# Blockwise linear attention and a two-layer product on one core: two more block products in seven multiplications, copies into the second bank, and loads that cast

## The chip, the cores and the metric

The kernel runs on one core of a Trainium2 chip. The core has a matrix engine (TensorE, PE in the profile; its weight loads are listed as PEld), three engines for everything else (VectorE or DVE, ScalarE or ACT, GpSimd or POOL), a queue engine (SyncE or SP), and 16 DMA engines that move data between the chip's memory (HBM) and the on-chip memory (SBUF). Products are written to eight banks of a small accumulator memory (PSUM, 2 KB per partition and bank). The metric is the device time of one execution, in microseconds.

## The reference

Inputs are q, k, v of 4 batches, 8 heads, 768 positions and 64 features, a decay per head, and two weight matrices. Cut to what matters:

```python
for b in range(12):                       # blocks of 64 positions
    intra = (qb @ kb.T) * Dmask           # lam ** (i - j) for i >= j
    out_b = intra @ vb + (qb * lam_pow) @ kv_state
    kv_state = lam ** 64 * kv_state + (kb * rev_pow).T @ vb
x = out.transpose(0, 2, 1, 3).reshape(3072, 512)
h = x @ w_in                              # 512 x 2048
return (h * sigmoid(h)) @ w_out           # 2048 x 512
```

## The kernel before

A block of the kernel is 128 positions (two of the reference's), so there are 6 blocks times 4 batches, 24 units of 128 rows, numbered by rank: block n of batch b is 4n + b from block 2 on, and blocks 0 and 1 of a batch stand together as units 0 to 7. Attention works on sets of two units: sets 0 to 3 are the paired blocks 0 and 1 of one batch, sets 4 to 11 are blocks 2 to 5, two batches each.

Per set the kernel loads k, q and v as float32 (`load_set`, L338, on SP's queue, 512 KB each, pieces of 256 bytes from block 2 on), casts k and q to bfloat16 (`cast`, L587, four quarter casts of 128x512 per set on ACT or DVE, into a buffer `kq`), scales v (`scale_v`), and turns k and q to feature-major form `kqT`. Sets 0 to 3 are turned on PE by transposes against an identity (eight transposes into one bank, then two copies out of it). Sets with `si >= TURNED` (4) are turned by a DMA transpose on SP's queue (`dma_turn`, L621). Then a burst of small matmuls gives states and scores (`first_part`), DVE masks the scores and updates the running state, and a second burst (`second_part`) gives the attention output, which DVE scales into `xt`, the right-hand side of the first product. From set 6 on, the second part of one set and the first part of the next go in one burst, which needs six PSUM banks at once.

The first product (`product1`, L813) multiplies w_in with one block of the four batches: 16 column blocks, four matmuls of 512 columns each, and a silu on ACT into tiles `g`. The last block (5) has a form with fewer multiplications instead (`product1_spared`, L906): both operands are split 2x2, seven products of sums take the place of eight products (Strassen's scheme in Winograd's form). Sums of weight quarters (`sums_of_w_in`) and of xt (T1 to T4) are made on DVE. In each of four column groups the seven products go to two banks, P and R. Products that are needed twice are copied from P to SBUF (`keep`) and added later by DVE (`total_of`).

The second product has a plain form, one unit at a time (`product2_plain`, L849, four pieces of four matmuls of 512 columns), for the first PLAIN units, and the seven-product form (`product2` and `products_of`, from L1010) for four units at a time, in pieces of sixteen matmuls of 256 columns. Sums of the left operand are on DVE, the fourth on POOL (`BY_POOL`); sums of w_out quarters are made once, and one of them (T1) overwrites a quarter of w_out, so it comes after all plain products. The last four units are done in two halves.

The order on all engines is made ahead of time by `Planner.order`, which simulates the engines: each task has a key (what is due first), an assumed duration on each engine that may do it, and buffers out of pools of fixed size (`POOLS`). A ready task goes to an engine if no other engine would end it earlier by the simulated times. `L320` in the profile is the helper of all tensor_tensor operations, `L313`, `L315` and `L317` that of copies on ACT, DVE and POOL. Keys of attention are LEAD (6.5) ranks ahead of its unit's first product. POOL's DMA issues (the weight loads, which cast to bfloat16) are chained in a fixed order, each held back by a one-column "gate" copy that waits for a load on SP's queue. Pools that matter here: eight banks; six `att` tokens, which limit the banks that attention and the pairs P, R hold at a time (a pair takes two); six `rb` buffers of 4 KB per partition for raw loads; three `kq`.

Of the kernel before, what the change touches and what calls it, by code (L numbers as in the profile page):

```python
# [37 lines left out]
class Planner:  # L38

    LAT = {"PE": 0.23, "ACT": 0.06, "DVE": 0.06, "POOL": 0.08, "SP": 0.0}  # L40
    BEGIN = {"PE": 0.8, "ACT": 8.3, "DVE": 4.5, "POOL": 4.7, "SP": 0.8}
    FIRST, LAST, AHEAD = {"SP": 1.9, "ACT": 1.15, "POOL": 2.5}, 1.0, 0.75
# [13 lines left out]
    def order(self):  # L56
# [63 lines left out]
        while len(out) < len(self.tasks):  # L120
# [9 lines left out]
            for e in free:  # L130
# [8 lines left out]
                while ready[e]:  # L139
# [12 lines left out]
                    mine = now + t.on[e]  # L152
                    if any(max(free[o], now) + d < mine - 1e-9 for o, d in t.on.items() if o != e):
                        kept.append((key, i, t))
                        continue
# [33 lines left out]
def kernel(  # L189
# [10 lines left out]
    nc = tc.nc  # L200
# [16 lines left out]
    FRESH, TURNED, ALONE, LEAD = 4, 4, 6, 6.5  # L217
    SEQUENCE = "s0 i0 s1 i1 i2 s2 i3 o0 s3 o1 o2 o3 s4"
    POOLS = dict(bank=8, ra=3, rb=6, kq=3, kqT=3, vd=3, st=3, xe=6, xf=3, y=2, yf=2,
                 xt2=2, xt4=2, g=18, s=12, m=3, osb=3, one=3, two=4, att=6)  # L220
    BY_POOL, IN_BY_POOL, PLAIN, SPARED = (4,), (), 8, 1
# [116 lines left out]
    def load_set(key, si):  # L338
        n, b = sets[si][0]
        nb = 2  # L340
        rs = [Buf("ra" if si in (0, 3) else "rb") for _ in range(3)]
# [11 lines left out]
        for i in range(3):  # L353
            ts.append([add((key, i), {"SP": 0.55}, lambda e, i=i: go(e, i), bufs=[rs[i]], nbytes=0.524,
                           kind=WIDE if n < PAIRED else SMALL, late=0.3 if si < FRESH else 3.0)])
# [54 lines left out]
    def key_of(si):  # L410
        u = rank[sets[si][0]]
        return u - 4.0 if sets[si][0][0] == 0 else u - LEAD
# [145 lines left out]
    def prepare(si):  # L558
# [7 lines left out]
        o.kq, o.kqT, o.vd, o.st = Buf("kq"), Buf("kqT"), Buf("vd"), Buf("st")  # L566
# [6 lines left out]
        def kq_of():  # L573
            return tile_of(o.kq, [128, nb, 2, NP, 2, 64], BF16, "kq")

        def kqT_of():
            return tile_of(o.kqT, [128, nb, 2, NP, U], BF16, "kqT")
# [9 lines left out]
        def cast(e, j, i):  # L587
            src = rs[i].tile[:, j * H:j * H + H, :].rearrange("p (m h) d -> p m h d", h=2)
            dst = kq_of()[:, j, i]
            copy(e, dst, src)  # L590

        ck = [[add((s - 1.0, i), {"DVE": 0.43, "ACT": 0.63}, lambda e, j=j, i=i: cast(e, j, i), deps=(lk, lq)[i],
                   bufs=[rs[i], o.kq]) for i in range(2)] for j in range(nb)]
        after("k", [t for ts in ck for t in ts])
# [10 lines left out]
        if si < TURNED:  # L605
            for j in range(nb):
                bank = Bank(fills=False)

                def turn(e, j=j, bank=bank):
                    t = tile_of(bank, [128, 2, NP, U], BF16, "tr")  # L610
                    for i in range(2):
                        for m in range(NP):
                            nc.tensor.transpose(t[:, i, m, :], kq_of()[:, j, i, m], ident)

                tr = add((s - 0.7, j), {"PE": 0.46}, turn, deps=ck[j], bufs=[bank, o.kq])
                for i in range(2):
                    o.turned.append(add((s - 1.0, 2), {"DVE": 0.43, "ACT": 0.6},
                                        lambda e, j=j, i=i, bank=bank: copy(e, kqT_of()[:, j, i], bank.tile[:, i]),
                                        deps=[tr], bufs=[bank, o.kqT]))
        else:  # L620
            def dma_turn(e):  # L621
                nc.sync.dma_start_transpose(kqT_of().rearrange("p b i m s -> p (b i m) s"),
# [550 lines left out]
```

## Time and profile before

| | |
|---|---|
| median of 3 runs | 208.62 us (208.38 to 209.31) |
| the profiled execution | 207.82 us, of which the profiled span is 206.1 us |
| TensorE busy | 187.0 us, 91% of the span |
| VectorE busy | 134.8 us, 65% |
| ScalarE busy | 107.4 us, 52% |
| GpSimd busy | 52.4 us, 25% |
| read from and written to HBM | 27.27 MB and 6.29 MB |

A page of the profile gives the busy time of each engine, the chain of work that ended last followed back from the end, the costliest groups of instructions by line and tile, and the DMA issues. "Idle before" a group is the time that its engine stood still ahead of it, with what ended that wait. Matmuls are pipelined and each record includes its way through the array, so the mean of a record (322 ns for a group) is longer than the step from one matmul to the next; steps are read from the chain, where sixteen matmuls of 256 columns take 1.75 us. The mean granted clock of TensorE is 0.989 of full speed.

### The profile page before, as it was taken

How to read it: one execution, taken by the hardware profiler on the slowest of the kernel's cores; microseconds unless marked ns; L12 is line 12 of the kernel's file. 1: busy time of each engine (PE TensorE's matmuls, PEld its weight loads, DVE VectorE, ACT ScalarE, POOL GpSimd, SP SyncE). 2: the span in 40 equal slices, each digit the busy share in tenths (PEclk: the TensorE clock that was granted, in tenths of full speed). 3: DMA queues.
4: the chain of work that ended last, by engine and by line, in shares of the span. 5: the costliest groups of instructions: out<-in, count | busy, mean ns of one | idle time of the engine just before them, and what ended most of it. 6: DMA issues, size and time to landing. Idle time of an engine off the chain costs nothing.

```text
span 206.1 us, 5719 instructions
## 1 busy us (share of the span) xinstructions
PE 187.0 (91%) x2445; PEld 132.9 (64%) x2464; DVE 134.8 (65%) x249; ACT 107.4 (52%) x195; POOL 52.4 (25%) x76
## 2 busy tenths in 40 slices
PE   0459399999999999999999999998999999999993
PEld 0347288786667565544578648474675778888882
DVE  6488632767950467716989953999758995665411
ACT  3637267874336453375734492745615453766420
POOL 7231400401130111222565013346003221222200
PEclk9999889999999999999999999999999999999999
DMA  3999999999999999999999999905101110102213
GB/s 99 292 253 260 228 222 265 235 199 214 228 238 249 156 216 231 238 219 195 263 213 234 203 213 240 244 7 117 39 3 54 51 54 0 54 0 102 88 52 118
DMA packets 88617, 33.92 MB, mean 165 GB/s; under 512 B 67088, under 2 KB 87568, under 8 KB 88592
## 3 DMA queue, kind: packets, MB, share of 16 engines
q1 hardware_dynamic: 79232, 23.60, 57.3%
q0 software_dynamic: 4224, 4.19, 12.2%
q10 hardware_dynamic: 5136, 5.77, 8.7%
q8 instruction: 19, 0.31, 0.7%
q14 instruction: 6, 0.05, 0.1%
HBM read 27.27 MB, written 6.29 MB: 163 GB/s over the span
## 4 chain that ended last, share of the span: by engine, by line
PE 82%; DMA 8%; DVE 7%; issue 1%; ACT 0%; POOL 0%; POOLq 0%; DVEq 0%
PE h_ps L830 31%; PE o_ps L1072 22%; PE o_ps L861 13%; PE h_ps L944 6%; DMA w_in_bf<-in_moe_w_in_dram 5%; DMA raw<-in_k_dram 3%; PE x_ps L687 2%; DVE s L320 2%; PE tr L442 2%; DVE g L320 1%; PE d_ps L647 1%; PE x_ps L679 1%; PE st_ps L657 1%; PE x_ps L538 1%; DVE kq L315 1%
## 5 line engine op out<-in xcount | busy, mean ns | idle before, releaser
L830 PE MATMUL h_ps<-xt,w_in_bf 128*128 128x256 bf16 (+1 forms) x439 | 75.7, 322 | 4.7 <-DMA w_in_bf<-in_moe_w_in_dram 3.3
L839 ACT ACTIVATE g<-h_ps 128x512 bf16<-128x512 f32 x80 | 47.1, 594 | 45.7 <-PE h_ps L830 45.0
L830 PEld LDWEIGHTS <-w_in_bf 128*128 128x128 bf16 x448 | 43.7, 99 | 30.1 <-DMA w_in_bf<-in_moe_w_in_dram 3.5
L861 PE MATMUL o_ps<-w_out_bf,g 128*128 128x512 bf16 x118 | 29.7, 379 | 0.6 <-issue 0.2
L320 POOL TENSOR_TENSOR s<-g,s 128x512 bf16<-128x512 bf16 x16 | 19.0, 1188 | 43.1 <-DVE s L320 26.8
L320 DVE TENSOR_TENSOR st<-st_ps,tri 128x512 bf16<-128x512 f32 x32 | 20.5, 681 | 11.2 <-PE st_ps L657 11.2
L1072 PEld LDWEIGHTS <-g 128*128 128x128 bf16 x256 | 24.9, 98 | 4.4 <-ACT g L839 0.3
L320 DVE TENSOR_TENSOR xt<-x_ps,lam_xe 128x512 bf16<-128x512 f32 x24 | 15.9, 699 | 15.2 <-PE x_ps L687 9.5
L1072 PEld LDWEIGHTS <-s 128*128 128x128 bf16 x192 | 18.7, 98 | 2.6
L861 PEld LDWEIGHTS <-g 128*128 128x128 bf16 x128 | 12.1, 98 | 12.0
L320 POOL TENSOR_TENSOR vd<-raw,lam_v 128x512 bf16<-128x512 f32 x10 | 13.3, 1334 | 25.1 <-DMA raw<-in_v_dram 19.7
L313 ACT ACTIVATE kq<-raw 128x512 bf16<-128x512 f32 x27 | 16.2, 621 | 2.1 <-DMA raw<-in_q_dram 1.6
L320 DVE TENSOR_TENSOR osb<-o_ps,m 128x512 f32<-128x512 f32 (+1 forms) x15 | 8.7, 583 | 10.9 <-ACT m L313 6.8
L1072 PE MATMUL o_ps<-wsum,g 128*128 128x256 bf16 x128 | 15.3, 272 | 0.0
L1072 PE MATMUL o_ps<-w_out_bf,s 128*128 128x256 bf16 x128 | 15.3, 273 | 0.0
L442 PE MATMUL tr<-ident,kq 128*128 128x128 bf16 x64 | 7.0, 260 | 8.8 <-POOL gate L331 6.9
L1072 PE MATMUL o_ps<-w_out_bf,g 128*128 128x256 bf16 x128 | 15.0, 273 | 0.0
L320 DVE TENSOR_TENSOR s<-g 128x512 bf16<-128x512 bf16 x16 | 8.2, 510 | 10.4 <-ACT g L839 6.6
L313 ACT ACTIVATE m<-o_ps 128x512 f32<-128x512 f32 (+1 forms) x14 | 7.0, 503 | 11.4 <-PE o_ps L1072 11.4
L320 DVE TENSOR_TENSOR vd<-raw,lam_v 128x512 bf16<-128x512 f32 x14 | 9.2, 681 | 5.0 <-DMA raw<-in_v_dram 5.0
L313 ACT ACTIVATE osb<-o_ps 128x512 f32<-128x512 f32 (+1 forms) x12 | 6.7, 562 | 10.4 <-PE o_ps L861 6.5
L315 DVE CAST kq<-raw 128x512 bf16<-128x512 f32 x21 | 9.1, 451 | 3.8 <-DMA raw<-in_k_dram 2.0
(88 smaller groups left out, 215.1 us busy)
## 6 DMA issues: line engine op xcount, KB each, us to landing
raw<-in_k_dram SPq DMA_DIRECT2D x12, 512.0 KB, 8.2
raw<-in_q_dram SPq DMA_DIRECT2D x12, 512.0 KB, 8.5
raw<-in_v_dram SPq DMA_DIRECT2D x12, 512.0 KB, 8.0
out_dram<-osb ACTq DMA_DIRECT2D x20, 256.0 KB, 3.6
w_in_bf<-in_moe_w_in_dram POOLq DMA_DIRECT2D x4, 512.0 KB, 10.0
w_out_bf<-in_moe_w_out_dram POOLq DMA_DIRECT2D x4, 512.0 KB, 11.7
out_dram<-osb ACTq DMA_DIRECT2D x4, 128.0 KB, 1.7
out_dram<-osb SPq DMA_DIRECT2D x4, 128.0 KB, 1.7
```

Source lines behind the costliest of these rows:

```text
L313: nc.scalar.activation(o, i, AF.Copy)
L315: nc.vector.tensor_copy(o, i)
L320: (nc.vector if e == "DVE" else nc.gpsimd).tensor_tensor(o, a, b, op=op)
L442: nc.tensor.transpose(t[:, m, a], o.kq_of()[:, i, m, a], ident)
L538: nc.tensor.matmul(t[rh, m], lhsT=o.vd_of()[r, 2 * m + h, a, :], rhs=o.st_of(h)[r, m, a], start=m == 0 and a == 0, stop=True, skip_group_c ...
L647: nc.tensor.matmul(d_of(c)[rp, j, m, :], lhsT=o.kq_of()[r, j, 0, m, p, :], rhs=o.vd_of()[r, j, 2 * m + p, :], start=j == 0 and m == 0, sto ...
L687: nc.tensor.matmul(x_of(c)[:, j, m, :], lhsT=o.xe[c].tile[:, (bs[0] + j) % 2, m, :], rhs=o.kqT_of()[:, j, 1, m, halves[c]], start=False, s ...
L830: nc.tensor.matmul(t[:, j, :], lhsT=w_in_bf[:, ko, 128 * (m1 + j):128 * (m1 + j) + 128], rhs=xt[gi].tile[:, ko, :], start=(ko == 0), stop= ...
L839: nc.scalar.activation(t[:, half * per:half * per + per], bank.tile, AF.Silu)
L861: nc.tensor.matmul(t, lhsT=g.tile[:, j, 128 * gp:128 * gp + 128], rhs=w_out_bf[:, ko, :], start=(ko == 0), stop=(ko == KO - 1))
L944: nc.tensor.matmul(t[:, j, :], lhsT=W[w]()[:, k2, f:f + 128], rhs=X(r)[:, k2, :], start=first and j == 0 and k2 == 0, stop=True, skip_grou ...
L1072: nc.tensor.matmul(t[:, i_, :], lhsT=src(j)[:, k2, 128 * r:128 * r + 128], rhs=W[w]()[:, 2 * j + k2, :], start=first and i_ == 0 and j == ...
```

## The change

There are seven parts.

1. `SPARED` goes from 1 to 2: block 4's first product also has the seven-product form. The sums of w_in get the key `SUMS_ON` (9.0, before: 16) and wait for the v scalings of ranks below 16 and for the casts of sets 0 to 5. A pool `sp` of two takes the place of the two `att` tokens of a pair: at most two column groups are in work at a time.
2. `PLAIN` goes from 8 to 4: units 4 to 7 have the seven-product form of the second product.
3. The first partial product is copied from bank P to bank R, and the second product adds onto it there (`first=False`), so that it waits for the copy. In the first product this is so for every pair, and silu then reads bank R itself; the wide tile and one add go. In the second product it is so for units 12 to 23 (`ONTO`), where the result is copied out of R instead of added.
4. k and q of sets 6 to 11 (blocks 3 to 5, `CASTING`) are loaded by DMAs on POOL's queue that cast to bfloat16, straight into the kq tile, which now lies in an `rb` buffer; the casts on ACT and DVE go. The kq tile has k and q outermost. Each set's two casting loads are chained on POOL behind the issue of the previous set's v load.
5. `TURNED` goes from 4 to 6: sets 4 and 5 (block 2) are turned on PE instead of by DMA.
6. The planner adds 0.2 us to DVE's time where it compares engines (`BIAS`), and some assumed durations of DVE sums are raised.
7. For units 4 to 7 two tokens of `two` are held instead of four. (`HURRY` is 0.0 and changes nothing.)

```diff
+    BIAS = {"DVE": 0.2}
...
-                    mine = now + t.on[e]
+                    mine = now + t.on[e] + self.BIAS.get(e, 0.0)
...
-    FRESH, TURNED, ALONE, LEAD = 4, 4, 6, 6.5
+    FRESH, TURNED, ALONE, LEAD = 4, 6, 6, 6.5
...
-    BY_POOL, IN_BY_POOL, PLAIN, SPARED = (4,), (), 8, 1
+    BY_POOL, IN_BY_POOL, PLAIN, SPARED = (4,), (), 4, 2
+    CASTING, SUMS_AFTER, HURRY, SUMS_ON, HOLD, ONTO = 6, 16, 0.0, 9.0, 1, 12
...
+            elif si >= CASTING and i < 2:
+                tl = tile_of(rs[0], [128, 2, 2, NP, 2, 64], BF16, "kq")
+                nc.gpsimd.dma_start(out=tl[:, i].rearrange("p b m h d -> p (b m h) d"), in_=x[i])
...
+            if si >= CASTING and i < 2:
+                t = pool_task(add((key, i), {"POOL": 0.8}, lambda e, i=i: go(e, i), bufs=[rs[0]], nbytes=0.524, kind=CAST,
+                                  prior=pool_last[-1:] + raw[si - 1][1][2], late=2.0))
...
-        o.kq, o.kqT, o.vd, o.st = Buf("kq"), Buf("kqT"), Buf("vd"), Buf("st")
+        o.kq, o.kqT, o.vd, o.st = rs[0] if si >= CASTING else Buf("kq"), Buf("kqT"), Buf("vd"), Buf("st")
...
-        on = rank[groups[-SPARED][0]] - 4.0
+        on = SUMS_ON
...
-            held = [P, R, Buf("att"), Buf("att")]
+            held = [P, R, Buf("sp")]
...
             m1 = product(0, P, "A11", "B11", True, [])
-            b1, c1 = keep("kqT", [m1])
-            m2 = product(1, R, "A12", "B21", True, [])
-            e11 = total_of(lambda w=wide_of: w()[:, :, lo], wide, b1, [m2, c1])
+            c1 = add((u0 - eager, 5), {"ACT": 0.6, "DVE": 0.69}, lambda e, P=P, R=R, f=bank_of: copy(e, f(R), f(P)), deps=[m1], bufs=[P, R])
+            m2 = product(1, R, "A12", "B21", False, [c1])
+            s11 = silu((low, lo), lambda R=R, f=bank_of: f(R), [m2], [R])
...
         m1 = product(0, P, "A11", "B11", True, [])
-        b1, c1 = keep(0, [m1])
-        m2 = product(1, R, "A12", "B21", True, [])
-        e11 = result(0, lo, R, b1, [m2, c1])
+        if u0 >= ONTO:
+            c1 = add((s - eager, 5), {"ACT": 0.17 + 0.215 * np_, "DVE": 0.15 + 0.27 * np_},
+                     lambda e: copy(e, bank_of(R), bank_of(P)), deps=[m1], bufs=[P, R])
+            m2 = product(1, R, "A12", "B21", False, [c1])
+            e11 = result(0, lo, R, None, [m2])
+        else:
+            b1, c1 = keep(0, [m1])
+            m2 = product(1, R, "A12", "B21", True, [])
+            e11 = result(0, lo, R, b1, [m2, c1])
```

More of the change, by code (lines that the diff above doesn't have):

```diff
@@ L151, in order @@
                         continue
-                    mine = now + t.on[e]
-                    if any(max(free[o], now) + d < mine - 1e-9 for o, d in t.on.items() if o != e):
+                    mine = now + t.on[e] + self.BIAS.get(e, 0.0)
+                    if any(max(free[o], now) + d + self.BIAS.get(o, 0.0) < mine - 1e-9 for o, d in t.on.items() if o != e):
                         kept.append((key, i, t))
@@ L340, in load_set @@
         nb = 2
-        rs = [Buf("ra" if si in (0, 3) else "rb") for _ in range(3)]
+        rs = [Buf("rb") if si >= CASTING and i == 0 else None if si >= CASTING and i == 1 else Buf("ra" if si in (0, 3) else "rb")
+              for i in range(3)]
         ts = []
@@ L1051, in product2, with products_of @@
         for part in ((0,), (1,)) if last else ((0, 1),):
-            products_of(units, s, A, part, last, eager)
-    def products_of(units, s, A, part, last, eager):
+            products_of(units, s, A, part, last, eager, u0)
+    def products_of(units, s, A, part, last, eager, u0):
         np_ = len(part)
         P, R = Buf("bank"), Buf("bank")
-        held = [P, R] + [Buf("two") for _ in range(2 * np_)]
+        held = [P, R] + [Buf("two") for _ in range(2 if u0 == PLAIN and HOLD else 2 * np_)]
         late = part[0] * 2 / 7 if last else 0.0
```

80 lines of the change are left out of this document (42 added, 38 removed).

## The prediction

> **What bounds the kernel now.** I read the page first (busy times, then the chain of work that ended last), then that chain in order of time, then busy times by stretch, and last the DMA issues.
>
> The page's busy row and its chain:
>
> ```profile
> span 206.1 us, 5719 instructions
> PE 187.0 (91%) x2445; PEld 132.9 (64%) x2464; DVE 134.8 (65%) x249; ACT 107.4 (52%) x195; POOL 52.4 (25%) x76
> PE 82%; DMA 8%; DVE 7%; issue 1%; ACT 0%; POOL 0%; POOLq 0%; DVEq 0%
> ```
>
> 82% of the time that set the end is TensorE work; DMA's 8% has one place, seen in the chain in order of time:
>
> ```profile
> 13.71 10.23 DMA w_in_bf<-in_moe_w_in_dram
> 23.94 0.05 issue
> 23.99 3.41 PE h_ps L830 x16
> ...
> 28.42 0.45 PE tr L442 x8
> ...
> 99.81 0.86 PE o_ps L861 x4
> 100.67 0.86 PE h_ps L830 x4
> ...
> 183.73 1.75 PE h_ps L944 x16
> 185.48 1.75 PE o_ps L1072 x16
> ...
> 190.28 12.24 PE o_ps L1072 x112
> 202.55 0.42 DVE osb L320
> ```
>
> Until 23.94 PE waits for the first weights. From then to 202.55 it is one queue of matmuls. The same lines give the prices: a 512-column matmul 0.86/4 = 0.216 us, a 256-column one 1.75/16 = 0.109, a turn of eight transposes 0.45. Busy times by stretch (columns: PE, PEld, DVE, ACT, POOL busy, clock, DMA share, GB/s):
>
> ```profile
> 62.00:94.00 32.00, 31.63 (x405) 18.38 (x411) 14.31 (x25) 17.08 (x30) 5.17 (x5) 1.00 1.05 218
> 94.00:129.00 35.00, 34.78 (x590) 23.17 (x583) 27.51 (x49) 19.10 (x34) 12.82 (x12) 1.00 1.22 222
> 129.00:141.00 12.00, 11.23 (x155) 6.93 (x156) 11.73 (x20) 7.03 (x13) 4.84 (x5) 1.00 0.48 104
> 161.00:190.30 29.30, 29.25 (x255) 24.85 (x255) 21.40 (x39) 16.66 (x28) 7.07 (x6) 1.00 0.13 46
> ```
>
> PE has almost no idle time; the only visible hole, 0.77 us, lies in 129 to 141, where DVE is 11.73 of 12 busy. Over the ten-microsecond stretches from 30 to 200 PE's idle time adds up to 1.9 us. The DMA engines are full to about 130 as well, but PE does not wait for them after 24. The issues, with size and time to landing:
>
> ```profile
> raw<-in_k_dram SPq DMA_DIRECT2D x12, 512.0 KB, 8.2
> w_in_bf<-in_moe_w_in_dram POOLq DMA_DIRECT2D x4, 512.0 KB, 10.0
> w_out_bf<-in_moe_w_out_dram POOLq DMA_DIRECT2D x4, 512.0 KB, 11.7
> kqT<-kq SPq DMA_TRANSPOSE x8, 6.8
> ```
>
> So the price of an edit is what it adds to or takes from PE's queue, unless it opens a hole there.
>
> **The change part by part, on PE.**
> Block 4's first product: 16 column blocks by 4 matmuls of 512 columns, 64 x 0.2157 (3.451/16, the mean of the 0.86 pieces) = 13.8 us, become 4 x 7 x 4 = 112 of 256 columns, 112 x 0.1093 (12.24/112) = 12.2. Gain 1.6.
> Units 4 to 7's second product: 4 x 16 = 64 of 512 columns become 7 x 16 = 112 of 256. Gain 1.6.
> TURNED goes from 4 to 6, so the two sets of block 2 are turned on PE and no longer by DMA: 2 x 2 turns of eight, 4 x 0.45 = 1.8. Loss 1.8.
> Sum: -1.6 - 1.6 + 1.8 = -1.4 us.
>
> **Off PE.** Casts: 24 of the 48 go (rows: 0.451 on DVE, 0.621 on ACT), about 13 us less on the two engines together. Added: 8 copies of turned tiles (0.42 or 0.60), 4; for block 4, 12 bank copies (0.595 on ACT, 0.69 on DVE), 7.5, 8 adds of 0.686, 5.5, and 4 sums of xt (0.42 to 1.38), 2.6; for units 4 to 7, 12 DVE sums at 0.51, 6, three copies and three adds, 4, less four evacuations of 0.56; four POOL sums of 1.19. Block 5 loses four adds of 0.686. Net some 12 us more on two engines that are busy 242 of 412 us. I cost it at nothing: PE's queue hides it, as it hides 21.40 us of DVE in the 29.3 from 161. If that cover is gone, as from 129 to 141, it costs what DVE has too much in that stretch; the casts that stand there leave at the same time (twelve on both engines from 94 to 129, four on ACT up to 141), so I take no new hole.
>
> The bias of 0.2 us against DVE only shifts work of either engine to ACT and POOL. It can move the start: POOL's gate copy at 13.59, which releases the weight load that PE waits for at 23.94, stood behind a 0.39-us state copy on POOL. Without that copy the start comes 0.4 earlier; with another state copy ahead of it, which waits for the state of 15.84 to 16.26, 2.7 later. I take 0, the row as it is: the first choices are made by engines that are free.
>
> The w_in sums (eight DVE instructions of 0.68 to 0.78, from 144 to 158 now) are moved ahead by seven ranks. They are still due before the first S product, and DVE has 0.87 busy of 10 us from 60 to 70, so nothing.
>
> m2 now waits for the copy c1, in eight pairs of first products and in the second products of units 12 to 23. Behind m2 on PE stand whatever pieces were ordered next, and they wait too. From below: nothing; from above, 8 x 0.6 + 2 x 0.6 + 2 x 0.4 = 6.8 us if no other piece stands between. I take nothing: c2 and c3 are the same hand-off today, and from 161 to 190 PE idles 0.05 us beside them. The sum that follows, s11, replaces an add and half a wide activation.
>
> The queues: SP loses twelve loads and two transposes. POOL gains twelve issues; its eight of today take 0.75 to 0.80 us each, so 9.3 us on an engine busy 25%, and what stands behind an issue (v scalings of 1.04, state copies, the fourth sums) starts that much later. A POOL issue for a buffer that is still held stops all of these; the bound is one buffer's wait. The row says nothing of 2,048 short pieces (the weight loads have 512 of 2 KB): SP's own issues of such loads take 2.1 us (median). So 0.75 to 2.1 each; I take 0.75, the same queue. In landing: 8.2 to 11.7, off PE's path while the slack below holds.
>
> The DMA engines: from 62 to 142 SP's queue was in use 91.3% of the time (73 us) for 18 loads and 7 transposes, 2.9 each. Two transposes fewer are about 5.8 us (estimate); casting loads write half the bytes, so from equal to half. Loads end some 6 to 12 us earlier, which alone gives PE nothing.
>
> **Sum.** The profiled execution took 207.82 (span 206.10 and 1.72 around it): 207.82 - 1.4 = 206.4. The median of the runs shown is 208.62, 0.8 above it, so 207.2.
>
> **Rivals.**
> First, the holes close too: earlier loads and fewer casts relieve 129 to 141. At most all 1.9 us of idle goes: 205.3. For it: that hole ends with DVE's xt. Against: block 4's adds come into the same stretch.
>
> Second, on the other side: the casting loads come late. In the trace the transposes of sets 6 to 11 were issued at 82.87, 90.45, 101.27, 112.16, 122.64 and 140.27; with 6.8 to landing, PE's bursts at 93.88, 102.40, 112.59, 125.53, 133.9 and 150.34 stood 3.3 to 6.6 us later, 4.7 in the mean. The plan's allowance for late landing is 3.0 us for SP's loads and 2.0 for the casting ones, so 3.7 remain. A landing as slow as w_out's (11.7 - 8.1 = 3.6) is just covered. If POOL also needs 2.1 per issue, two issues bring 2.7 more, and a burst waits 2.6: 209.8. And DVE and POOL hold each other up in the trace: a v scaling on POOL took 2.81 at 55.87 (median 1.04) beside DVE's sums and casts. Issues held by 1.8 each bring 3.5, and a burst waits 3.4: 210.6. It decides from 2.4 in all (1.4 to the old time and 1.0 beyond it). Against: all eight issues of today stayed within 0.75 to 0.96, some beside DVE's masks, and the DMA engines get less to move. I side with the issue rows.
> The Trainium skill, page SBUF — State Buffer (section SBUF: two separate sides), speaks for the hold: a DMA issued from GpSimd has its descriptors written by GpSimd, which can't write them while VectorE runs in a two-port mode. By that rule the sum would be 210.6, by the issue rows 207.2; the scaling of 2.81 agrees with a hold between the two engines, but no row shows an issue held.
>
> Third: block 4's pairs collide with attention. A pair's chain (four products of 0.44, three copies of 0.6, two adds of 0.69) is 4.9 us for 3.05 of PE work; two pairs hold four of eight banks, and a burst of block 5 wants six. Draining a pair costs PE up to 1.9. With both bursts, 3.7: 210.9; it decides when both are hit. For it: in the old order block 4's first product (140.6 to 167) overlaps the bursts at 150 and 157. Against: bursts rank ahead of the product and their loads come earlier.
>
> Fourth: the gain is eaten by small waits at c1, near 208.4.
>
> **How the numbers follow.** A measurement of this kernel can tell about 0.5% (1.0 us) from no change. The forecast (206.6 to 207.9 by itself): 0.42, of which 0.31 below 207.6. Closing holes: 0.19. Late casts (209.8 to 210.6): 0.16. Bank collisions: 0.15. Small waits: 0.08. Faster 0.31 + 0.19 = 0.50, same 0.11 + 0.08 = 0.19, slower 0.31. The range: 205.3 (all idle gone) to 211.0 (both bursts drained); several late bursts, or a start late by 2.7 with a collision, are left out above.
>
> **What would show it.** Right: h_ps of block 4 and the early second products as 256-column matmuls at 0.109, four more turns of eight transposes at 0.45, 24 casts gone, PE idle about 2 us from 30 to 200, last product 1.4 earlier. Wrong: PE waiting for raw or kqT (late casts), for h or m copies beside x_ps bursts (banks), clock below 1 after 30, POOL issues of 2 us, or a first weight load that lands after 24.

## The result, and the profile after

| | before | after |
|---|---|---|
| median | 208.5 us (6 runs, 207.04 to 209.31) | 216.05 us (6 runs, 214.39 to 216.36) |
| ratio to before | | 1.039 (95% interval 1.035 to 1.043) |
| the profiled execution, its span | 207.82, 206.1 us | 216.36, 214.7 us |
| PE idle from 30 to 200 us | 1.83 us | 9.38 us |
| packets of the two loading queues (q1 is SP's, q0 POOL's) | 79,232 and 4,224 | 50,304 and 28,992 |

The change makes the kernel 3.9% slower. The forecast was 207.2, faster, with a range up to 211.0; the time lies outside it.

The page of the kernel after, its busy row and its chain by engine:

```profile
span 214.7 us, 6034 instructions
PE 189.4 (88%) x2592; PEld 146.2 (68%) x2592; DVE 143.4 (67%) x255; ACT 111.7 (52%) x207; POOL 74.1 (35%) x97
PE 57%; DMA 24%; SPq 7%; DVE 7%; issue 2%; ACT 0%; DVEq 0%; ACTq 0%
```

PE's part of the chain fell from 82% to 57%, and DMA's rose from 8% to 24%. The same stretches as before the change, in the same columns (PE, PEld, DVE, ACT, POOL busy, clock, DMA share, GB/s):

```profile
62.00:94.00 32.00, 25.23 (x414) 17.42 (x412) 25.85 (x39) 14.94 (x26) 19.54 (x18) 0.99 1.61 186
94.00:129.00 35.00, 32.87 (x553) 23.36 (x554) 26.97 (x43) 13.93 (x24) 19.26 (x19) 0.91 1.25 161
129.00:141.00 12.00, 12.00 (x168) 8.01 (x166) 9.38 (x18) 5.29 (x9) 2.18 (x2) 1.00 0.30 67
161.00:190.30 29.30, 29.30 (x271) 26.25 (x270) 19.41 (x35) 19.05 (x35) 6.29 (x6) 1.00 0.13 46
```

From 129 on PE has no idle time at all, better than before. The loss lies in 62 to 129, above all in 62 to 94: PE 25.23 busy against 31.63. There the DMA share went up, from 1.05 to 1.61, while the bytes moved went down, from 218 to 186 GB/s. The chain in order of time, between 56 and 102 (start, length, what):

```profile
56.37 16.19 DMA raw<-in_v_dram
...
72.58 0.69 DVE vd L322
73.28 2.05 DVE w_out_bf L322 x2
...
78.26 0.10 DVE vd L322
78.35 1.00 issue
79.35 16.04 DMA kqT<-kq
...
95.43 0.65 PE st_ps L669 x24
96.08 5.55 PE o_ps L1086 x32
```

A v load on SP's queue took 16.19 us to land (median before: 8.0). After it come v scalings and other work on DVE, then the DMA transpose of set 6 on the same queue, which took another 16.04 (median before: 6.8, longest 8.7). PE's own timeline shows the end of it:

```profile
88.83 0.45 PE L659 MATMUL d_ps<-vd,kq 64*64 64x64 bf16 x32
95.43 0.65 PE L669 MATMUL st_ps<-kqT 64*64 64x64 bf16 x32 [6.16 <-DMA kqT<-kq]
96.01 3.60 PE L1086 MATMUL o_ps<-wsum,s 128*128 128x256 bf16 x16
```

Before, the burst of set 6 began at 93.81, with its transpose issued at 82.87, and its scores followed without a wait:

```profile
93.81 0.45 PE L647 MATMUL d_ps<-vd,kq 64*64 64x64 bf16 x32
94.09 0.44 PE L657 MATMUL st_ps<-kqT 64*64 64x64 bf16 x32
```

Now it begins at 88.83, five microseconds earlier in PE's order, and its transpose lands at 95.39. PE stands still for 6.16 us. Then it runs slowly: sixteen matmuls of 256 columns take 3.60 instead of 1.91, and the chain's 32 take 5.55 where 32 x 0.1093 is 3.50, so 2.05 more.

The account, by the two pages' totals: PE's idle time over the span grew by 6.2 (25.3 against 19.1). From 30 to 200 it grew by 7.55, of which 6.16 is this one wait; before 30 it fell by 1.4. PE's busy time grew by 2.4 (189.4 against 187.0), of which 2.05 is the slow clock behind the wait. Together that is 8.6, by which the span grew. The -1.4 of the prediction's sum can't be read from the busy time, which also holds slow matmuls at the start of both kernels (of 256 columns: before, sixteen took 3.41 at 23.99; after, eight took 1.66 at 17.90 and 0.97 at 24.30).

POOL's timeline has the casting loads (the three lines are those of k; each is followed by q's). The page's transfers by queue (packets, MB, share of the engines) and the median landing of each kind come after it:

```profile
61.26 1.21 POOL L355 DMA_DIRECT2D kq<-in_k_dram  x1 [3.31 <-DVE vd L322]
...
67.50 1.15 POOL L355 DMA_DIRECT2D kq<-in_k_dram  x1
...
80.06 1.22 POOL L355 DMA_DIRECT2D kq<-in_k_dram  x1
```

```profile
q1 hardware_dynamic: 50304, 16.26, 39.6%
q0 software_dynamic: 28992, 7.34, 35.3%
...
raw<-in_v_dram SPq DMA_DIRECT2D x12, 512.0 KB, 11.4
...
kq<-in_k_dram POOLq DMA_DIRECT2D x6, 256.0 KB, 8.5
kq<-in_q_dram POOLq DMA_DIRECT2D x6, 256.0 KB, 10.7
...
kqT<-kq SPq DMA_TRANSPOSE x6, 9.0
```

These pairs of issues belong to sets 7, 8 and 9. They are in flight while SP's queue moves v loads and the transpose that PE needs first. POOL's queue carries 28,992 packets instead of 4,224; 12 casting loads make 24,768 of them, 2,064 each.

Part of the delay stood in SP's own queue. Set 6's casting loads were issued at 53.48 and 54.69 and landed 7.8 and 10.7 later, the second at 65.4. The transpose that reads them was issued 14 us after that, behind four v loads:

```profile
56.37 22.87 SPq L357 DMA_DIRECT2D raw<-in_v_dram  x4
79.35 9.81 SPq L634 DMA_TRANSPOSE kqT<-kq  x1
```

Counted among the twelve v loads, the last two of the four are those of sets 7 and 8. This order alone does not cost the time: in three kernels of the experiments below that lose nothing, the same four loads stand ahead of the transpose, which is issued at 75.80 to 76.13.

### The profile page after: what moved, and what is told of

The parts are those of the page before. It is cut to its first block, busy times and chain, and to the rows that moved or that the text cites. A ratio compares the mean times of both kernels' runs of the same rounds, so it can differ in the third digit from the quotient of the medians.

```text
span 214.7 us, 6034 instructions
## 1 busy us (share of the span) xinstructions
PE 189.4 (88%) x2592; PEld 146.2 (68%) x2592; DVE 143.4 (67%) x255; ACT 111.7 (52%) x207; POOL 74.1 (35%) x97
## 3 DMA queue, kind: packets, MB, share of 16 engines
q1 hardware_dynamic: 50304, 16.26, 39.6%
q0 software_dynamic: 28992, 7.34, 35.3%
## 4 chain that ended last, share of the span: by engine, by line
PE 57%; DMA 24%; SPq 7%; DVE 7%; issue 2%; ACT 0%; DVEq 0%; ACTq 0%
PE o_ps L1086 26%; DMA raw<-in_v_dram 16%; PE h_ps L956 11%; PE h_ps L842 11%; DMA kqT<-kq 7%; SPq L352 7%; PE o_ps L873 3%; DVE s L322 1%; PE x_ps L699 1%; DVE vd L322 1%; DVE g L322 1%; DVE w_out_bf L322 1%; PE st_ps L669 1%; DMA out_dram<-osb 1%; PE x_ps L691 1%
## 5 line engine op out<-in xcount | busy, mean ns | idle before, releaser
L842 PE MATMUL h_ps<-xt,w_in_bf 128*128 128x256 bf16 (+1 forms) x384 | 62.4, 313 | 3.0 <-DMA w_in_bf<-in_moe_w_in_dram 1.5
L851 ACT ACTIVATE g<-h_ps 128x512 bf16<-128x512 f32 x64 | 37.6, 595 | 27.6 <-PE h_ps L842 27.0
L842 PEld LDWEIGHTS <-w_in_bf 128*128 128x128 bf16 x384 | 37.4, 99 | 20.9 <-issue 1.8
L322 POOL TENSOR_TENSOR s<-g,s 128x512 bf16<-128x512 bf16 x20 | 23.9, 1193 | 66.3 <-DVE s L322 36.8
L1086 PEld LDWEIGHTS <-g 128*128 128x128 bf16 x320 | 31.2, 98 | 5.5 <-issue 1.0
L1086 PEld LDWEIGHTS <-s 128*128 128x128 bf16 x240 | 24.3, 102 | 4.3
L322 DVE TENSOR_TENSOR h<-h_ps,m 128x512 f32<-128x512 f32 x16 | 11.0, 690 | 10.3 <-PE h_ps L956 5.4
L322 DVE TENSOR_TENSOR osb<-o_ps,m 128x512 f32<-128x512 f32 (+1 forms) x14 | 8.5, 610 | 11.7 <-ACT m L315 9.0
L873 PE MATMUL o_ps<-w_out_bf,g 128*128 128x512 bf16 x64 | 15.3, 379 | 0.0
L322 POOL TENSOR_TENSOR vd<-raw,lam_v 128x512 bf16<-128x512 f32 x10 | 11.4, 1146 | 9.7 <-PE x_ps L691 3.8
L956 PEld LDWEIGHTS <-wsum 128*128 128x128 bf16 x128 | 12.4, 98 | 1.6
L980 ACT ACTIVATE g<-h 128x512 bf16<-128x512 f32 x16 | 10.0, 628 | 4.5 <-DVE h L322 4.5
## 6 DMA issues: line engine op xcount, KB each, us to landing
raw<-in_v_dram SPq DMA_DIRECT2D x12, 512.0 KB, 11.4
w_out_bf<-in_moe_w_out_dram POOLq DMA_DIRECT2D x4, 512.0 KB, 10.7
kq<-in_q_dram POOLq DMA_DIRECT2D x6, 256.0 KB, 10.7
```

The lines of the kernel that those rows point to most:

```text
L322: (nc.vector if e == "DVE" else nc.gpsimd).tensor_tensor(o, a, b, op=op)
L842: nc.tensor.matmul(t[:, j, :], lhsT=w_in_bf[:, ko, 128 * (m1 + j):128 * (m1 + j) + 128], rhs=xt[gi].tile[:, ko, :], start=(ko == 0), stop= ...
L851: nc.scalar.activation(t[:, half * per:half * per + per], bank.tile, AF.Silu)
L873: nc.tensor.matmul(t, lhsT=g.tile[:, j, 128 * gp:128 * gp + 128], rhs=w_out_bf[:, ko, :], start=(ko == 0), stop=(ko == KO - 1))
L956: nc.tensor.matmul(t[:, j, :], lhsT=W[w]()[:, k2, f:f + 128], rhs=X(r)[:, k2, :], start=first and j == 0 and k2 == 0, stop=True, skip_grou ...
L980: nc.scalar.activation(o, src(), AF.Silu)
```

## The experiments

Our theory after the result: casting loads of later sets share the DMA engines with SP's queue and hold back what is needed first; the planner, which assumes a cost for each transfer, does not know it. The rivals: a casting load is dear in itself; the new products or the copies into the second bank open the holes; the turns on PE cost what was predicted or more.

### What a casting load costs by itself

The kernel only moves data: its output is all zeros, and the reference's computation is left out. It has seven stages, each waiting for the one before.

```diff
+    for i, t in enumerate(sp):
+        sp_load(t, i)                 # float32, SP's queue, pieces of 256 bytes
...
+    for i, t in enumerate(cast):
+        pool_load(t, 4 + i)           # the same pieces, cast to bfloat16, POOL's queue
...
+    for i in range(N):
+        sp_load(both_s[i], 12 + i)    # four of each side by side
+        pool_load(both_c[i], 16 + i)
...
+    for i in range(N):
+        pool_load(last[i], 20 + i)
+        if i < 2:
+            turn(turned2[i], wide[i]) # two transposes beside four casting loads
```

> Only transfers, in seven stages one after the other (no attention, no products; the output is zeros): four float32 loads of short pieces on SP's queue; four casting loads of short pieces on POOL's queue; four POOL loads of short pieces without a cast; four casting loads in 4-KB runs; four of SP's and four casting loads side by side; two transposes alone; two transposes beside four casting loads. Theory A (the casting load itself is dear on the DMA engines): the profile of the changed kernel gives (35.3% x 214.7 - 12.2% x 206.1)/12 = 4.2 us of all 16 engines per casting load, SP's queue 2.4 per load; so about 16 us for the second stage against 9 to 10 for the first, and the fifth stage near their sum, 25. The third stage says whether the cast or POOL's queue is dear, the fourth whether the short pieces are. Theory B (the loads are cheap but issued late behind POOL's other work): the second stage is no longer than the first. Rival within A: side by side the two queues overlap, so the fifth stage is as long as its longer part, 16.

Busy times by stretch (columns: DVE, POOL, clock, DMA share, GB/s), the stages of four SP loads, four casting loads, four POOL loads without a cast, and four of each kind:

```profile
2.00:13.70 11.70, 2.55 (x14) 0.00 (x0) 1.00 0.95 179
14.50:25.20 10.70, 0.94 (x7) 4.71 (x4) 1.00 1.53 98
26.00:38.60 12.60, 0.92 (x6) 4.61 (x4) 1.00 0.77 166
48.30:68.90 20.60, 1.34 (x13) 4.60 (x4) 1.00 1.43 153
```

| stage | time, us | packets |
|---|---|---|
| four float32 loads on SP's queue | 11.6 | 8,256 |
| four casting loads on POOL's queue | 10.7 | 8,256 |
| four POOL loads without a cast, same pieces | 12.6 | 576 |
| four casting loads that read runs of 4 KB | 8.3 | 576 |
| four SP loads beside four casting loads | 20.6 | 16,512 |
| two transposes alone, and beside four casting loads | 6.9, and 16.1 | |

A casting load alone is no dearer than SP's: 10.7 against 11.6 us for four, where theory A had 16 against 9 to 10. It is not cheaper in packets either, though it writes half the bytes: 2,064 each, one for each piece of 256 bytes and a few more. Side by side the two kinds need 20.6 us, nearly their sum of 22.3, as theory A had it: little is gained from the second queue. In the steady part of that stage (58 to 62) each queue moved some 415 packets per microsecond by the trace's packets, half and half, so SP's queue, which alone had 853 to 868 (from 8 to 11), runs at half its speed. There are worse microseconds: 1,035 against 102 at 56. In the changed kernel, from 84 to 87, while set 6's transpose is in flight, POOL's queue moved 860 to 908 packets per microsecond and SP's 146 to 280. The two transposes landed 4.9 us after their issue alone and 9.4 beside casting loads.

The Trainium skill, page DMA: Bandwidth & Descriptors (section Queues, rings and completion order), says that each DMA engine takes turns between the queues that have work for it, a packet at a time. The steady 415 and 415 agree; the uneven microseconds are not explained by it.

### The changed kernel with long runs in the casting loads

Here the casting loads read as many bytes as in the changed kernel, in the same order and into the same tiles, but from other positions of k and q: 128 runs of 4 KB instead of 2,048 pieces. The values are therefore not those of the reference.

```diff
-                nc.gpsimd.dma_start(out=tl[:, i].rearrange("p b m h d -> p (b m h) d"), in_=x[i])
+                src = (k, q)[i]
+                run = bass.AP(tensor=src.tensor, offset=src.offset + (si - CASTING) * 128 * 1024, ap=[[1024, 128], [1, 1024]])
+                nc.gpsimd.dma_start(out=tl[:, i].rearrange("p b m h d -> p (b m h d)"), in_=run)
```

> The changed kernel in its own order, but each of the twelve casting loads reads 128 runs of 4 KB (other positions of k and q than it should) in place of 2,048 pieces of 256 bytes; bytes, cast, queue and waits stay. Theory A: the 6.2-us wait for set 6's transpose and the halved clock behind it (2.05 us) go, so 206 to 208.5, where the forecast of 207.2 stood. Theory B (order, POOL's waits for buffers) and theory C (the pairs of products, the copies or the bank limits cost the time): 213 or more.

206.79 us against 207.61, ratio 0.997 (0.993 to 1.001). The whole loss is gone, with the same planned order and the same number of DMAs. POOL's queue has 5,952 packets, and in PE's timeline the burst of set 6 finds its transpose landed:

```profile
87.73 0.45 PE L661 MATMUL d_ps<-vd,kq 64*64 64x64 bf16 x32
88.00 0.44 PE L671 MATMUL st_ps<-kqT 64*64 64x64 bf16 x32
```

The scores follow the state without a wait. The cost of the short pieces is the difference of the two medians, 216.05 and 206.79: about 9.3 us, over different chips, or 4.2% by the two ratios. Long runs also shorten POOL's issues, from 1.15 to 1.22 us to 0.53 to 0.61. That this matters here is not ruled out by this run alone, but the chain of the changed kernel has no POOL work in it.

### Long runs for sets 7 to 9 alone

```diff
+                if si in (7, 8, 9):
+                    src = (k, q)[i]
+                    run = bass.AP(tensor=src.tensor, offset=src.offset + (si - CASTING) * 128 * 1024, ap=[[1024, 128], [1, 1024]])
+                    dst = tl[:, i].rearrange("p b m h d -> p (b m h d)")
```

> The changed kernel in its own order; only the casting loads of sets 7, 8 and 9 read 4-KB runs (at other positions than they should), six of the twelve; those of sets 6, 10 and 11 keep their 256-byte pieces. These six are issued from 61 to 82, while PE's next burst waits for set 6's transpose. If what hurts is that loads needed later take packets from SP's queue (theory A3), set 6's transpose lands in time: 207 to 210, all or nearly all of the 8-us loss gone with half the loads cured. If each casting load makes its own set late (A4), set 6 stays late: 212 or more.

207.62 us against 207.54, ratio 1.001 (0.998 to 1.005). Set 6, whose transpose PE waited for, keeps its own casting loads in 2,048 pieces each, and still the wait is gone, because the loads of sets 7 to 9 stand in the way no longer. Its transpose is issued at 75.83 instead of 79.35, and PE meets it at 86.81:

```profile
86.54 0.44 PE L665 MATMUL d_ps<-vd,kq 64*64 64x64 bf16 x32
86.81 0.44 PE L675 MATMUL st_ps<-kqT 64*64 64x64 bf16 x32
```

So it is not the set's own loads that come late, as the prediction's second rival had it. Loads for bursts that come nine microseconds later and more (set 7's begins at 95.89) take the DMA engines from what is needed now.

### The same casting loads, with other assumed costs

The planner's table of transfers says how long each kind keeps the DMA engines. Only two entries are changed: a casting load from 14 to 21 where it shares the engines (31 to 21 where it runs alone), a transpose from 50 per 1,024 to 18.5 per 378. The order then comes out otherwise.

```diff
-(256, 14.0, 31.0)
+(256, 21.0, 21.0)
...
-(1024, 50.0, 50.0)
+(378, 18.5, 18.5)
```

> The changed kernel with two of the planner's assumed transfer costs set to what the run of transfers alone showed: side by side, SP's and POOL's short-piece loads moved 410 packets per us each, one packet for one; so a casting load is charged 21 per 256 bytes, shared or alone (before: 14 shared, 31 alone), and a transpose 18.5 per packet of 378 bytes (before: 50 per 1,024). All else stays; the order comes out another. Theory A1 (the plan mispriced the sharing, so loads were ordered where the DMA engines could not carry them): most of the loss goes, 207 to 210. Theory A2 (casting loads in such small pieces cost too much wherever they stand): still 212 or more.

207.25 us against 207.54, ratio 0.999 (0.997 to 1.002): the loss is gone again, and here the loads are the changed kernel's own. The casting issues stand where they stood (53.39 to 109.17). The transposes are no faster, 13.2 us to landing in the median. The chain of this kernel has set 6's:

```profile
76.13 17.89 DMA kqT<-kq
```

It lands at 94.02, as late as in the changed kernel (95.39). But PE's order is another:

```profile
83.67 4.48 PE L842 MATMUL h_ps<-xt,w_in_bf 128*128 128x512 bf16 x20
87.99 1.91 PE L1086 MATMUL o_ps<-wsum,s 128*128 128x256 bf16 x16
89.74 1.91 PE L1086 MATMUL o_ps<-w_out_bf,s 128*128 128x256 bf16 x16
91.48 1.89 PE L842 MATMUL h_ps<-xt,w_in_bf 128*128 128x512 bf16 x7
93.31 0.45 PE L659 MATMUL d_ps<-vd,kq 64*64 64x64 bf16 x32
94.06 0.45 PE L669 MATMUL st_ps<-kqT 64*64 64x64 bf16 x32 [0.31 <-DMA kqT<-kq]
```

Products that were ready fill the time, and the burst stands at 93.31 instead of 88.83. The late transpose costs 0.31. The loss of the change thus needs both: transfers that are slowed, and an order of PE's instructions that does not count on it. The five kernels side by side (landings are us from issue, from the DMA issues of that stretch):

| | before | after | long runs | long runs, 7 to 9 | recosted |
|---|---|---|---|---|---|
| v loads issued from 65 to 76 | 8.0 | 15.0 | 10.7 | 13.2 | 16.2 |
| set 6's transpose issued at | 82.87 | 79.35 | 75.80 | 75.83 | 76.13 |
| its landing | 6.8 | 16.0 | 9.0 | 10.8 | 17.9 |
| so landed at | 89.7 | 95.4 | 84.8 | 86.6 | 94.0 |
| PE is ready for it at | 94.09 | 89.27 | 88.00 | 86.81 | 93.75 |

A positive slack of 4.4 us before became a wait of 6.16. The packets account for most of the transpose's landing and for its later issue. Not all of the delay is theirs: the first of the four v loads that the new order issues in a row, at 56 to 57, takes 14.5 and 15.7 with long runs too.

### The casting loads alone, in the kernel before

```diff
+    CASTING = 6
...
+            elif si >= CASTING and i < 2:
+                tl = tile_of(rs[0], [128, 2, 2, NP, 2, 64], BF16, "kq")
+                nc.gpsimd.dma_start(out=tl[:, i].rearrange("p b m h d -> p (b m h) d"), in_=x[i])
```

> The kernel before with part 4 alone (casting loads for sets 6 to 11, straight into the kq tile). Theory A: slower by 4 to 12 us (212 to 220), with PE waiting for a transpose between 80 and 140; with eight DMA transposes it can be worse than in the changed kernel. Theory C: within 1.5 us of 208.5.

221.06 us against 207.61, ratio 1.064 (1.058 to 1.070), above the 212 to 220 that were expected. Part 4 alone costs more than the whole change. Of PE's waits (us in all, times, longest) the one that is new:

```profile
PE st_ps L668 <- DMA kqT<-kq: 7.8, 3, 3.9
```

With TURNED at 4 there are eight transposes for the casting loads to slow (11.4 to landing in the median), and PE waits three times for them; its clock is 0.88 from 62 to 76 and 0.92 from 100 to 141.

### The change without casting loads

Sets 6 to 11 are loaded and cast as before (`CASTING` 12, so no set casts by DMA); the first products wait for the last sum of w_in, `wdone["S4"]`.

```diff
-    CASTING, SUMS_AFTER, HURRY, SUMS_ON, HOLD, ONTO = 6, 16, 0.0, 9.0, 1, 12
+    CASTING, SUMS_AFTER, HURRY, SUMS_ON, HOLD, ONTO = 12, 16, 0.0, 9.0, 1, 12
...
-            m1 = product(0, P, "A11", "B11", True, [])
+            m1 = product(0, P, "A11", "B11", True, wdone["S4"])
```

> The changed kernel without part 4: k and q of all sets come over SP's queue and are cast on ACT and DVE; all other parts stay. (The first product of block 4 also waits for the last sum of w_in, since its buffer is freed late.) Theory A: no wait for a transpose of 6 us; 207 to 210, PE's work 1.4 us below the kernel before, some of it given back because loads come later again. Theory C: 213 or more.

209.38 us against 207.61, ratio 1.009 (1.006 to 1.012). Without part 4 the loss shrinks to a quarter, but there is no gain: the other parts, by the prediction's sum worth -1.4 us, cost 1.8. A variant with four more turns, LEAD 6, EAGER 10, ONTO 8 and the recosted transposes was also tried:

> A try at a kernel that beats both: no casting loads (all k and q over SP's queue), blocks 2 and 3 turned on PE (TURNED = 8, four sets, 3.6 us of PE work in place of 1.8), the planner's transpose cost by packets, ONTO = 8, EAGER = 10, LEAD = 6; all else as in the changed kernel. By PE's queue +0.4 us on the kernel before (-3.2 + 3.6); four DMA transposes fewer. From 207 to 209.5; it wins only if it also has fewer holes than the 1.9 us of before.

209.76 us against 207.54, ratio 1.014 (1.008 to 1.021): slightly above its range, and no gain.

### The products alone

The kernel before, with one number changed each: `PLAIN` from 8 to 4 (units 4 to 7's second product), and `SPARED` from 1 to 2 (block 4's first product).

```diff
-    BY_POOL, IN_BY_POOL, PLAIN, SPARED = (4,), (), 8, 1
+    BY_POOL, IN_BY_POOL, PLAIN, SPARED = (4,), (), 4, 1
```

> The kernel before with the second part alone: PLAIN from 8 to 4, so that the second product of units 4 to 7 has the seven-product form; nothing else is changed, and no load casts. By the prediction's sum PE's queue loses 1.6 us and nothing else moves: the ratio to the kernel before is 0.992. Rival (the saving needs work that isn't there): the seven-product form needs the sums of w_out and of the left operand, three DVE adds and three copies per piece, at a time when PE has little else ready; PE's busy time falls by 1.6, but PE's idle time from 30 to 141 grows by more than that: ratio 1.00 to 1.02.

212.16 us against 207.44, ratio 1.021 (1.016 to 1.027). That is at the upper edge of what the rival had. By stretch, PE loses in the same part of the span as in the changed kernel (from 76 to 100 it is busy 19.48 of 24 us, before 23.73), with no casting load anywhere (columns: PE, PEld, DVE, ACT, POOL busy, clock, DMA share, GB/s):

```profile
70.00:77.00 7.00, 7.00 (x116) 5.96 (x117) 7.00 (x13) 4.11 (x8) 3.09 (x3) 1.00 1.02 223
77.00:84.00 7.00, 2.57 (x113) 1.79 (x111) 6.67 (x13) 2.37 (x4) 2.81 (x3) 0.78 1.04 213
```

DVE is busy 7.00 of 7.00 us, then 6.67 of 7.00, where the kernel before had 5.29 of 7.00 in the first. PE waits for DVE's states, copies and, for 2.37, its `xt`. In that stretch the clock is 0.78.

```diff
-    BY_POOL, IN_BY_POOL, PLAIN, SPARED = (4,), (), 8, 1
+    BY_POOL, IN_BY_POOL, PLAIN, SPARED = (4,), (), 8, 2
```

> The kernel before with the first part alone: SPARED from 1 to 2, so that block 4's first product has the seven-product form in the old arrangement (partial products kept in SBUF, two att tokens held per pair, the sums of w_in due four ranks before block 4's first product). By the prediction's sum the ratio is 0.992. Rival (bank and engine collisions): the pairs of block 4 hold att tokens and DVE just where block 5's bursts want them, so PE's idle time from 94 to 161 grows by 2 to 10 us: ratio 1.01 to 1.04.

216.74 us, ratio 1.044 (1.039 to 1.048). Here the loss is where blocks 4 and 5 meet:

```profile
141.00:151.00 10.00, 8.28 (x120) 6.83 (x119) 9.52 (x15) 2.42 (x4) 3.43 (x4) 1.00 0.43 110
151.00:161.00 10.00, 6.81 (x140) 5.53 (x131) 7.54 (x13) 2.42 (x4) 0.00 (x0) 0.83 0.13 44
```

DVE is at 9.52 of 10 and PE at 8.28; then PE waits 2.30 for `st`. In the changed kernel PE is busy 20.00 of 20.00 from 141 to 161. So something in the other parts removes what this part alone costs. The earlier sums, the tokens of the pool `sp`, the copies into the second bank and the casts that are gone can all do it; which of them does was not separated.

### The turns alone

```diff
-    FRESH, TURNED, ALONE, LEAD = 4, 4, 6, 6.5
+    FRESH, TURNED, ALONE, LEAD = 4, 6, 6, 6.5
```

> The kernel before with TURNED = 6 alone: block 2's two sets are turned on PE. By the prediction's rule (what is added to PE's queue is paid) 1.8 us slower: 210.3 against 208.5, a ratio of 1.009. Rival: the two DMA transposes gone let loads come earlier and pay it back, 208 to 209.

207.81 us against 207.54, ratio 1.003 (1.001 to 1.005): 0.6 us, where four turns at 0.45 had been put at 1.8. The four turns are there, and why they cost less is not separated: PE idles 2.25 us from 30 to 200 against 1.83, but it is busy 18.04 of the first 31 us instead of 17.32.

### Two attempts at a faster version

Both have the recosted transfers. The first gives up the second products of units 4 to 7 (`PLAIN` 8, LEAD 6):

```diff
-    FRESH, TURNED, ALONE, LEAD = 4, 6, 6, 6.5
+    FRESH, TURNED, ALONE, LEAD = 4, 6, 6, 6
...
-    BY_POOL, IN_BY_POOL, PLAIN, SPARED = (4,), (), 4, 2
+    BY_POOL, IN_BY_POOL, PLAIN, SPARED = (4,), (), 8, 2
```

> The changed kernel with the planner's assumed transfer costs as in the recosted plan, with LEAD 6 instead of 6.5 and PLAIN back at 8 (the second product of units 4 to 7 plain again). If the saving of units 4 to 7 is paid back by PE's idle time, this loses nothing by giving it up: 206.3 to 207.3 us, ratio 0.994 to 1.000. If the saving is real there, PE's queue is 1.6 longer and so is the time: ratio 1.005 to 1.01.

209.27 us against 207.44, ratio 1.006 (1.003 to 1.009). Against the recosted plan's 0.999 that is 0.7%, about 1.4 us, near the 1.6 by which PE's queue is longer. That speaks for a real saving of this part once its DVE work has cover; it is not shown, since LEAD differs too.

The second casts only sets 8 to 11 by DMA and turns sets 6 and 7 on PE:

```diff
-    FRESH, TURNED, ALONE, LEAD = 4, 6, 6, 6.5
+    FRESH, TURNED, ALONE, LEAD = 4, 8, 6, 6.5
...
-    CASTING, SUMS_AFTER, HURRY, SUMS_ON, HOLD, ONTO = 6, 16, 0.0, 9.0, 1, 12
+    CASTING, SUMS_AFTER, HURRY, SUMS_ON, HOLD, ONTO = 8, 16, 1.0, 9.0, 1, 12
```

> The changed kernel with casting loads only for sets 8 to 11 (CASTING 8), sets 6 and 7 turned on PE (TURNED 8), the two transfer costs of the recosted plan, HURRY 1.0 and EAGER 10; the first products wait for the last weight sum. Our theory (the loss is casting loads that take packets from the v loads and transposes needed first): the only transposes left are those of sets 8 to 11, at most one casting load runs ahead of a transpose that PE waits for, so the 6-us wait is gone. PE's queue has four turns more, 4 x 0.45 = 1.8 us, and 8 casts more stand on ACT and DVE; with the small gain of the recosted plan: 206.3 to 209.0 us, ratio 0.995 to 1.007. Rival (any casting loads beside SP's queue cost, wherever they stand): ratio above 1.015.

212.67 us against 207.36, ratio 1.025 (1.021 to 1.029), a miss for our theory's number. The number lies in the rival's range, but the trace does not bear the rival out: PE waits for no transpose (they land in 5.8 us in the median). Its longest waits behind the start name DVE, 2.6 us for `s` and 1.4 for `osb`:

```profile
92.00:102.00 10.00, 7.86 (x150) 6.09 (x151) 9.82 (x16) 1.70 (x4) 7.00 (x6) 0.83 1.37 184
102.00:112.00 10.00, 8.63 (x64) 6.05 (x63) 9.96 (x14) 4.03 (x7) 5.57 (x6) 1.00 0.98 107
```

DVE is full for twenty microseconds, with eight more casts and eight more copies of turned tiles to place than in the changed kernel. It is the next bound behind the transfers. No version tried beats the kernel before by more than a measurement can tell; the best are the recosted plan, 0.999, and the long runs, 0.997, whose values are not the reference's.

## Why the prediction was wrong

**The step that failed: the DMA engines.** It read "casting loads write half the bytes, so from equal to half. Loads end some 6 to 12 us earlier". In packets a casting load equals SP's own (2,064), which is one end of that bound; side by side the two kinds need nearly the sum of their times. What was left out is the order. Before, one queue took loads and transposes one after the other in the planned order. With two queues, the loads of sets 7 to 9 ran beside what set 6 still lacked, and SP's queue got half of the packets or fewer. What stayed on SP's queue landed later after its issue, not earlier: v 11.4 instead of 8.0, transposes 9.0 instead of 6.8, the one that decides 16.04. The prediction had written "off PE's path while the slack below holds" and then counted only the casting loads' own landing against that slack. The runs show it from both sides: long runs for sets 7 to 9 alone bring the time back, and so does an order of PE's work that comes to the burst later. The half of the step that speaks of the end came out: the last load on SP's queue was issued at 114.84 instead of 126.77. It gave PE nothing, as the prediction had said.

**Off PE, "I cost it at nothing: PE's queue hides it".** The amount was right: VectorE and ScalarE together were busy 255.1 us instead of 242.2, 12.9 more where some 12 were worked out. The price of nothing was not tested by the changed kernel, whose PE waits elsewhere, and wrong for the parts by themselves: +2.1% and +4.4% where -0.8% each was worked out, both with DVE full beside a waiting PE. The average of 65% for DVE does not show this. In 76 to 100 it was busy 13.82 of 24 us before, 23.41 in the recosted plan and 23.88 with long runs.

**PE's sum, -1.4.** The prices held (1.75 for sixteen of 256 columns, 0.45 for a turn). As time, the turns were over-priced: 0.6 instead of 1.8. With the loss taken away, the change stands at 0.997 or 0.999 of before, 0.1 to 0.7 us of the 1.4, and both intervals include none. PE's idle time from 30 to 200 is 4.0 us with long runs and 4.6 in the recosted plan against 1.83, so part of the saving turns into waits; how much is not settled, since the profiled executions of these two took 1.1 and 1.6 us more than their medians.

**m2 behind the copy c1, at 0.** Right: 29.30 of 29.30 from 161 to 190.3, 20.00 of 20.00 from 141 to 161.

**The start, at 0 (bounds -0.4 to +2.7).** PE waited 1.5 us for the first weights instead of 3.3 and was busy 18.75 of the first 31 us instead of 17.32: better than the bound of 0.4. The kernel with the turns alone has 18.04, so part of it is the turns that stand there. The prediction read that PE waits for the weights until 23.94; it was busy 10.32 of the first 24 us, and the wait was 3.34. What it left out is the clock: behind that wait sixteen matmuls of 256 columns took 3.41, in the chain that it shows, where later ones took 1.75 (clock 0.53 from 24 to 27.4). Behind the shorter wait of the changed kernel the clock stayed at 1.00.

**POOL's issues, 0.75 (bounds 0.75 to 2.1).** Measured 1.15 to 1.22, so 14.1 us for the twelve instead of 9.3. The loads alone show the same 1.17 without a cast and 0.565 for 128 runs: it goes by pieces. POOL also stood still before three of the issues, for 3.45, 3.31 and 2.89 us, the last until set 6's transpose had landed. The prediction had named such a wait for a buffer and counted nothing for it; what it cost was not measured.

**Landing of the casting loads, 8.2 to 11.7.** Right as medians, 8.5 and 10.7, though the slowest took 15.7; but what decided was the landing of others.

**The second rival (late casting loads, 209.8 to 210.6).** Its sign and its place (a burst that waits for its operands) were right. Its mechanism was not: no issue took longer than 1.22, set 6's own loads had landed 14 us before its transpose was issued, and the price was 6.16 for one burst and 2.05 for the clock, where it had 2.6 to 3.4 and no clock. The rule of the Trainium skill, page SBUF — State Buffer (section SBUF: two separate sides), which gave its upper end, was not seen at work: all twelve issues took 1.15 to 1.22, four of them between 80 and 99, in a stretch (76 to 100) where DVE was busy 20.61 of 24 us. Whether DVE was in a two-port mode there, no run shows.

**The first and third rival.** The hole from 129 to 141 did close (12.00 of 12.00, before 11.23), worth 0.77 and lost in the rest. The collision of block 4's pairs with attention did not come in the changed kernel. With block 4's products alone PE does wait there, beside a full DVE; whether the banks had a part in it was not separated.

What stays open: why the engines moved only some 300 to 530 packets per microsecond on the two queues from 88 to 92 in the changed kernel, against 830 in the measured mix, why the shares of the queues are uneven at times, and how much of the 1.4 us a better order could keep.

## What to carry to other kernels

A load that is moved to a second queue no longer waits its turn: before it is priced at nothing, ask what on the first queue is needed earlier, and measure the two side by side, since neither bytes nor the time of one alone told it here. Where an order is made ahead from assumed costs, a wrong cost of a transfer turns into a wait of the engine that follows the order to the letter; two entries of the table were worth 4.0% here (1.039 against 0.999). An engine's share over the whole span says little: price work off the critical path by its busy time in the stretch where it will stand.

## What the runs showed of the hardware

A cast in a DMA changes how it is cut: a POOL load of 2,048 pieces of 256 bytes is 144 packets without a cast and 2,064 with one. The packets alone do not set the time: four of the former took 12.6 us, four of the latter 10.7.

TensorE's clock fell after some short holes. In the last kernel of the experiments (columns as above) PE stood still for 2.64 us, to 94.14; the clock was 1.00 until 94 and reached its low 2 us after work had begun again:

```profile
92.00:94.00 2.00, 0.00 (x0) 0.00 (x0) 2.00 (x3) 0.32 (x1) 1.47 (x1) 1.00 1.85 126
94.00:96.00 2.00, 1.86 (x58) 1.56 (x62) 1.85 (x5) 0.00 (x0) 0.90 (x1) 0.82 1.29 244
96.00:98.00 2.00, 2.00 (x82) 1.83 (x73) 2.00 (x2) 0.00 (x0) 1.55 (x2) 0.50 1.51 95
```

So a hole can cost its own length and up to about 2 us more behind it (2.05 after the one of 6.16, 1.66 after the one of 3.34 in the kernel before). Its length alone does not decide: after 2.65 us, to 24.00, in the kernel with the second products alone, and after 2.31, to 23.32, in the one with the turns alone, the clock stayed at 1.00. In the kernel before, no hole from 30 on was longer than 0.8, and the clock stayed at 1.00 from there to 200. The Trainium skill, page TensorE: Matmul & The Clock Gate (section Part 1: The HAM clock gate), gives half rate after an idle window of about 3.4 us; these runs show it after holes of 2.64 and, with block 4's products alone, of 2.30 and 0.41 with little work about them (clock 0.83 from 151 to 161) too.
